# A recurrent attention block with routed rows: the order of scores and results, and who owns which PSUM banks

## The chip, the cores and the metric

The kernel runs on one core of a Trainium2 chip. The metric is the device time of one execution in microseconds. TensorE (PE) multiplies matrices and writes only to PSUM; VectorE (DVE) and ScalarE (ACT) read PSUM and work element by element; GpSimd (POOL) works element by element on SBUF; SyncE (SP) issues the transfers between HBM and SBUF. Each engine works through its own instructions in the order in which they were written, and waits when an operand or a buffer isn't ready.

## What is computed

Two blocks follow one another. The first is a recurrence over 768 steps for 4 batches and 8 heads of width 48. The second picks the 128 rows of highest score of each batch, sends them through a small network of two layers (384 to 1024 to 384) and adds the result, gated, to these rows.

```python
for t in range(S):
    kt, vt, rt, wt = (k[:, :, t], v[:, :, t], r[:, :, t], w[:, :, t])
    cur = np.einsum('bhd,bhe->bhde', u[None] * kt, vt)
    y[:, :, t] = np.einsum('bhd,bhde->bhe', rt, state + cur)
    state = wt[:, :, :, None] * state + np.einsum('bhd,bhe->bhde', kt, vt)
...
scores = np.einsum('bsd,d->bs', x, w_gate)      # x is y as (B, S, H*D)
out = x.copy()
for b in range(B):
    top_idx = np.argpartition(-scores[b], capacity)[:capacity]
    xe = x[b, top_idx]
    ye = np.maximum(xe @ w1, 0.0) @ w2
    g = 1.0 / (1.0 + np.exp(-scores[b, top_idx]))
    out[b, top_idx] = x[b, top_idx] + g[:, None] * ye
```

All data is fp32.

## The kernel before

**Chunks.** The 768 steps of a batch are cut into 6 chunks of 128, so there are N = 24 chunks, worked through one after the other. Within a chunk the recurrence becomes products of matrices: with the running products of the decays, r and k are scaled to R and K, "scores" are the products of K and R, "masked" leaves those of earlier steps, and the results are the masked scores times v plus R times the state at the chunk's start. The state is carried on to the next chunk of the batch with the products of k and v. The heads are handled as four pairs (HP = 4), two heads on the 128 partitions.

**Turns.** The program is written as turns, `turn(i)` for i from -2 to 24, in an order set by hand (`tc.manual_schedule()`). A turn works on several chunks: it makes R of chunk i+1, the decays and K's transposes of chunk i+2, masked scores and results of chunk i, rows of chunk i-1, and it compares the row scores of chunk i-2 with those of the batch so far. As each engine keeps the written order, an instruction that waits holds up everything of its engine that is written after it.

What a turn does, by name:

- `first_left`, `own_products`, `own_weights`, `own_values`, `own_results`: the term with u, for the step itself. Products on POOL; then, for each of 8 heads, a sum over 48 elements on ScalarE (L372), then times v on POOL and, for chunks 1 to 7, half of the heads on ScalarE (L385).
- `scaled` K (L349): VectorE takes K's transposes from PSUM and scales them.
- `compared(i-2)`: TensorE spreads a column of row scores into psW (ps_e, L533); VectorE compares with all earlier chunks of the batch (L535, longer with each chunk) and with the chunk itself (L539); ScalarE keeps the spread scores in "every" for later chunks (L544), except after the last chunk of a batch.
- `back(i)`: K turned back for the carry (L278), copied by ScalarE to kt (L414). Not for a batch's last chunk.
- `rows_back(i-1)`: the results turned back to rows (L278), copied by ScalarE to x (L452); `rows_out` adds the own term (POOL, L458) and stores the rows; `row_products` (POOL, L463) and `row_sums` (ScalarE, L468) give the row scores.
- `masked(i)` (VectorE, L404).
- `inputs_t(i+1, "R")` (L271) and `scaled` R on VectorE; `decays_t(i+2)` (L271 into psW).
- `range_check(i+2)` on ScalarE (L338); `carry_products(i)` (L488), for the first chunks copied by ScalarE to kvs (L494); `carry` makes the next state.
- `outputs_t(i)`: the results (L429, L437) into ps_yt, copied by ScalarE to yt (L442).
- `scores(i+1)` (L396) into psS, then `inputs_t(i+2, "K")` (L271).
- `scans(i+2)` on VectorE: running products of the decays from the right (L291) and the left (L302).

**The routed part.** When the last chunk of a batch has been compared, `mixture(b)` is taken up, a generator that stands in the turns' `mix(place=...)`: ranks (ps_r, L562), "picks" on VectorE (L580), "half" (ps_i, L587, the list of rows, then the gather of the rows), "mid" (the gathered rows transposed, ps_x, L611, copied to xeT), then the gate. The network itself is `forward`, of which `fed_in_turn` puts a few products (L647, L659) into each turn. The last batch's network stands behind the last turn, with TensorE almost alone.

**PSUM.** Of the 8 banks psW has one (decays, ps_e), psT two that are used in turn (transposes of R and K, back, rows, carry), psS two (scores), psV two (one tile for the results, and in between ps_r, ps_i and ps_x), and psM one (the network). A tile that is asked for from a pool waits until the readers of the tile that had its bank are done.

**Loads.** `loads(i+5)` at a turn's end asks for w, r, k and v some chunks ahead, into four buffers each, on SyncE's queue, on which the stores of rows stand too. The weights of the network come in seven pieces from turn 2 on.

Of the kernel before, what the change touches and what calls it, by code (L numbers as in the profile page):

```python
# [10 lines left out]
FP32 = mybir.dt.float32  # L11
# [7 lines left out]
L = 128  # L19
DP = 64  # L20
# [17 lines left out]
def kernel(  # L38
# [49 lines left out]

    AHEAD = S // L + 2

    FIRST = H * 5 // 8
    NDC = C // L
    NFC = F // L
# [11 lines left out]
    psW = ctx.enter_context(tc.tile_pool(name="psW", bufs=1, space=PSUM))  # L105
    psT = ctx.enter_context(tc.tile_pool(name="psT", bufs=2, space=PSUM))
    psS = ctx.enter_context(tc.tile_pool(name="psS", bufs=1, space=PSUM))
    psV = ctx.enter_context(tc.tile_pool(name="psV", bufs=1, space=PSUM))
    psM = ctx.enter_context(tc.tile_pool(name="psM", bufs=1, space=PSUM))

    chunks = [(b, ci) for b in range(B) for ci in range(NCH)]
# [5 lines left out]
    def crossed(j, q):  # L117
        return q ^ (j & 1)

    def half(q):  # L120
        return slice(DP * q, DP * q + DP)
# [296 lines left out]
    def outputs_t(t):  # L418

        n = t["n"]  # L420
        vt = v_bufs[n % NBUF]
        old = state.get(n)

        ps = psV.tile([L, 2, HP, L], FP32, tag="v", name="ps_yt")

        for j in range(HP):
            for c in (0, 1):
                q = crossed(j, c)
                nc.tensor.matmul(  # L429
                    ps[half(c), j % 2, j // 2, :], vt[:, 2 * j + q, :], t["sc"][:, q, j, :],  # L430
                    start=(j < 2), stop=(old is None), skip_group_check=True,
                )
        for j in range(HP if old is not None else 0):
            for c in (0, 1):
                q = crossed(j, c)
                rows = slice(DP * q, DP * q + DP)
                nc.tensor.matmul(  # L437
                    ps[DP * c:DP * c + D, j % 2, j // 2, :], old[rows, j, :],
                    t["R"][rows, j, :], start=False, stop=True, skip_group_check=True,
                )  # L440
        t["yt"] = lev.tile([L, 2, HP // 2, L], FP32, tag="yt", name="yt")
        nc.scalar.copy(out=t["yt"], in_=ps[:, :, 0:HP // 2, :])  # L442

    def rows_back(t, soon=False):
        y = dense(psT, "t", lambda j: t["yt"][0:DE, j % 2, j // 2, :], lambda j: crossed(j, 0))
        x = t["x"] = lev.tile([L, C], FP32, tag="x", name="x", bufs=3)
        xj = x.rearrange("p (j e) -> p j e", j=HP)
        if soon:
            vo = t.pop("vo").rearrange("p (j q) d -> p j (q d)", q=2)
            nc.vector.tensor_add(xj, y, vo)  # L450
        else:
            nc.scalar.copy(out=xj, in_=y)  # L452
# [28 lines left out]
    def carry_products(t):  # L481
        n = t["n"]
        if chunks[n][1] == NCH - 1:
            return
        t["kv"] = kv = psT.tile([L, HP, D], FP32, tag="t", name="ps_kv")
        for j in range(HP):
            for q in (0, 1):
                nc.tensor.matmul(  # L488
                    kv[half(q), j, :], t["kt"][:, j, q, :],
                    v_bufs[n % NBUF][:, 2 * j + q, 0:D], start=True, stop=True,  # L490
                )
        if n < AHEAD:
            t["kv"] = lev.tile([L, HP, D], FP32, tag="kvs", name="kvs")
            nc.scalar.copy(out=t["kv"], in_=kv)  # L494
# [22 lines left out]
    def compared(t):  # L517

        b, ci = chunks[t["n"]]
        if ci == 0:  # L520
            while len(against) > 1:
                mix()
            against[b] = (
                mod.tile([L, S - L], FP32, name="every", bufs=2),
                mod.tile([L, NCH, S], BF16, name="ahead", bufs=2),
                lost_bufs[b % 2],
            )
        every, ahead, lost = against[b]
        own = score[:, b, ci:ci + 1]
        lo, hi = ci * L, (ci + 1) * L  # L530

        ps = psW.tile([L, L], FP32, tag="w", name="ps_e")
        nc.tensor.transpose(ps, own.to_broadcast([L, L]), ident)  # L533
        if ci > 0:
            nc.vector.tensor_scalar(  # L535
                out=ahead[:, ci, 0:lo], in0=every[:, 0:lo], scalar1=own, scalar2=None,
                op0=ALU.is_ge, op1=ALU.add, accum_out=lost[:, ci, 0:1],
            )
        nc.vector.scalar_tensor_tensor(  # L539
            out=ahead[:, ci, lo:hi], in0=ps, scalar=own, in1=after_f,  # L540
            op0=ALU.is_ge, op1=ALU.mult, accum_out=lost[:, ci, 1:2],
        )
        if ci < NCH - 1:
            nc.scalar.copy(out=every[:, lo:hi], in_=ps)  # L544

    def mixture(b):

# [4 lines left out]


        every, ahead, lost = against[b]
        def room(shape, name):
            pool, tag = (psT, "t") if ended else (psV, "v")
            return pool.tile(shape, FP32, tag=tag, name=name)

        ps = room([L, NCH], "ps_r")
# [12 lines left out]
        for gi, (c0, n) in enumerate(groups):  # L572
# [9 lines left out]
                    op0=ALU.is_equal,  # L582
                )
            yield "half"
            ps = room([L, 2], "ps_i")
            for c in range(NCH):
                nc.tensor.matmul(  # L587
                    ps, pick[:, c, :], ids[:, b, c, :], start=(c == 0), stop=(c == NCH - 1)
# [45 lines left out]
    def forward(b, n, idx, xe, xeT, gate, gated):  # L634

        load_weights(len(weights) - NFC // 2)
        hid = mod.tile([L, NFC, L], FP32, name="hid")  # L640
        for f0 in range(0, NFC, 4):

            pool, tag = (psV, "v") if ended and f0 % 8 == 0 else (psM, "m")
            ps = pool.tile([L, 4, L], FP32, tag=tag, name="ps_h")
            for q in range(4):
                for dc in range(NDC):
                    nc.tensor.matmul(  # L647
                        ps[:, q, :], w1[:, dc, (f0 + q) * L:(f0 + q + 1) * L],
                        xeT[:, dc, :], start=(dc == 0), stop=(dc == NDC - 1),
                    )  # L650
                if q == 3:
                    nc.scalar.activation(out=hid[:, f0:f0 + 4, :], in_=ps, func=AF.Relu)  # L652
                yield q == 3

        load_weights(len(weights))
        pool, tag = (psV, "v") if b == B - 1 else (psM, "m")
        ps = pool.tile([L, C], FP32, tag=tag, name="ps_f")
        for fc in range(NFC):
            nc.tensor.matmul(  # L659
                ps, hid[:, fc, :], w2[:, fc, :], start=(fc == 0), stop=(fc == NFC - 1)  # L660
            )
            yield fc == NFC - 1
        while not gated:
            mix()
        ye = mod.tile([L, C], FP32, name="ye", bufs=2)
        nc.vector.scalar_tensor_tensor(  # L666
            out=ye, in0=ps, scalar=gate, in1=xe, op0=ALU.mult, op1=ALU.add
        )
        nc.gpsimd.indirect_dma_start(  # L669
            out=views[b][0:b + 1].rearrange("b s c -> (b s) c"),  # L670
            out_offset=bass.IndirectOffsetOnAxis(ap=idx[0:n, 0:1], axis=0),
            in_=ye[0:n], in_offset=None,
            bounds_check=(b + 1) * S - 1, oob_is_err=False,
        )
        yield True
# [5 lines left out]
    def step(f, n, *more):  # L681
        if 0 <= n < N:
            f(work.setdefault(n, dict(n=n)), *more)
# [38 lines left out]
    def turn(i):  # L722
        soon = i >= N - 1
        step(first_left, i + 1)
        if i < 1:
            step(scaled_aside, i + 1, "K", "right")
        step(own_products, i + 1)

        first = FIRST if feed or picked else 0
        step(own_values, i, range(first))  # L730
        step(carry, i - 1, work.get(i))
        if i > 0:
# [7 lines left out]
            sums.extend(check_sums())  # L740
        if i < N:
            step(compared, i - 2)
        step(back, i)
        step(rows_back, i - 1, soon)
        mix(place="half")
        if not soon:
# [13 lines left out]
        if i == -2:  # L760
            warm(2)
        step(range_check, i + 2)
        if not soon:
            step(row_sums, i - 1)
        if i == -1:
            spread(u_bc.rearrange("p h d -> p (h d)"), u_row)
            step(own_weights, i + 1)
        step(carry_products, i)
        step(outputs_t, i)
        step(scores, i + 1)  # L770
        step(inputs_t, i + 2, "K", k_bufs)
        if i == -2:
            warm(1)
# [3 lines left out]
        fed_in_turn(PIECES - PIECES // 2, 1 if i == N - 1 else 0)  # L777
        if i == N - 1:
            step(compared, i - 1)
        step(scans, i + 2)  # L780
        mix(place="end")
        if i > -2:
            loads(i + 5)
# [3 lines left out]
    with tc.manual_schedule():  # L787
        warm(6)
        for i in range(-2, N + 1):
            turn(i)  # L790

        ended.append(True)
        mix(1000)
        mixing.append([mixture(B - 1), "picks"])
        step(compared, N - 1)
        fed(1)
        mix(2)
        wide = checked(sums)
        fed(1)
        mix()  # L800
        fed(NFC - 2)
        mix(2)
        fed(2)
        mix(1000)
        fed(1000)
        outside = nc.values_load(wide, min_val=0, max_val=1)


    def general(gen):
        u_t = gen.tile([D, H], FP32, name="u_t")  # L810
        nc.sync.dma_start(out=u_t, in_=u.rearrange("h d -> d h"))
        for b in range(B):
# [27 lines left out]
            for c in range(NCH):  # L840
                x = lev.tile([L, C], FP32, tag="x", name="x", bufs=3)
                nc.sync.dma_start(out=x, in_=out[b, c * L:(c + 1) * L, :])
                t = dict(n=b * NCH + c, x=x)
                row_scores_soon(t)
                compared(t)
            for _ in mixture(b):
                pass
            fed(1000)
# [30 lines left out]
```

## Time and profile before

| | |
|---|---|
| time, median of 3 runs | 206.23 us (203.56 to 206.38) |
| profiled run | 204.75 us, span 203.0 us |
| left scan (L302) of turn 2, 5, 8, 11, 14, 17, 20 starts at | 26.75, 46.59, 67.41, 90.68, 112.63, 134.30, 156.25 us |
| busy: TensorE, VectorE, POOL, ScalarE | 184.6, 161.1, 139.5, 127.8 us |
| transfers of r, k, v, w, each chunk | 192 KB each, 4.2 to 5.0 us from issue to landing |

The left scan is the last step of VectorE in a turn, so the distance of two of these starts is the length of the turns between them. Batch 0's rows are ranked in turns 7 to 9; from then on the network's products stand in the turns. The last scan starts at 163.48 us; after the last turns the network of the last batch follows. A matrix product in the profile is pipelined with the next: four transposes of 280 ns each take 0.44 to 0.66 us together.

### The profile page before, as it was taken

What the parts mean: (1) busy time and instruction counts of PE and PEld (TensorE: products, weight loads), DVE (VectorE), ACT (ScalarE), POOL (GpSimd) and SP (SyncE); (2) the same over time, 40 slices, a digit from 0 to 9 for tenths busy, and PEclk for the clock granted to TensorE, in tenths of its full rate; (3) what the DMA queues carried; (4) which work ended last, traced back from release to release, by engine and by line L of the source; (5) the groups of instructions that cost most, each with busy time, mean ns of one, the idle gap of its engine ahead of it and who ended that gap; (6) DMA issues with size and microseconds to landing.
All of it is one profiled execution on the core that took longest, in us unless ns stands there. A gap on an engine that the chain in (4) does not pass through costs nothing. (4 is left out here: it accounts for less than half of the span.)

```text
span 203.0 us, 7183 instructions
## 1 busy us (share of the span) xinstructions
PE 184.6 (91%) x2673; PEld 151.2 (74%) x2673; DVE 161.1 (79%) x348; ACT 127.8 (63%) x653; POOL 139.5 (69%) x186
## 2 busy tenths in 40 slices
PE   7898889887998979999999999999999999899980
PEld 2577768665776859879787789888788798776940
DVE  6999898999999696898999888998999885861010
ACT  5486879877994485688674576678646758410300
POOL 8689888876886966876686889697667797111302
PEclk9999999999999799999999999999999999999999
DMA  7999999999999989699776875958973141111101
GB/s 117 163 166 153 148 191 199 242 190 240 194 210 218 253 179 175 163 212 157 163 153 93 179 158 131 183 120 123 157 156 91 30 119 44 39 42 42 39 8 44
DMA packets 105390, 28.86 MB, mean 142 GB/s; under 512 B 100482, under 2 KB 104580, under 8 KB 105348
## 3 DMA queue, kind: packets, MB, share of 16 engines
q1 hardware_dynamic: 104304, 26.65, 73.4%
q0 software_dynamic: 512, 1.57, 2.3%
q8 instruction: 23, 0.38, 0.9%
q14 instruction: 19, 0.16, 0.3%
q10 hardware_dynamic: 532, 0.10, 0.2%
HBM read 22.81 MB, written 5.51 MB: 139 GB/s over the span
## 5 line engine op out<-in xcount | busy, mean ns | idle before, releaser
L372 ACT ACTIVATE rk<-rk 128x48 f32<-128x48 f32 x192 | 44.1, 240 | 0.0
L372 ACT ACTIVATION_READ_ACCUMULATOR rk<-rk 128x1 f32 x192 | 37.8, 197 | 0.0
L458 POOL TENSOR_TENSOR x<-x,vo 128x384 f32<-128x384 f32 x22 | 22.1, 1006 | 20.1 <-ACT x L452 20.0
L302 DVE TENSOR_TENSOR_SCAN left<-ps_w,from_left 128x511 f32<-128x511 f32 x24 | 30.7, 1280 | 0.9
L404 DVE TENSOR_TENSOR sc<-ps_s,before_f 128x1024 f32<-128x1024 f32 x24 | 29.2, 1218 | 1.4 <-PE ps_s L396 1.4
L291 DVE TENSOR_TENSOR_SCAN right_buf<-ps_w,from_right 128x511 f32<-128x511 f32 x24 | 29.1, 1211 | 0.6 <-PE ps_w L271 0.6
L429 PE MATMUL ps_yt<-sc,v_buf 128*64 128x128 f32 x384 | 26.6, 282 | 0.7 <-ACT xeT L613 0.5
L647 PE MATMUL ps_h<-xeT,w 128*128 128x128 f32 x192 | 25.0, 278 | 1.2 <-ACT hid L652 1.2
L396 PE MATMUL ps_s<-R,K 64*64 64x128 f32 x768 | 25.5, 270 | 0.0
L364 POOL TENSOR_TENSOR rk<-rk,u_bc 128x384 f32<-128x384 f32 x24 | 24.0, 1000 | 1.2 <-DVE alls L297 0.7
L647 PEld LDWEIGHTS ps_h<-xeT,w 128*128 128x128 f32 x192 | 22.9, 192 | 2.4 <-ACT hid L652 1.9
L361 POOL TENSOR_TENSOR rk<-r_buf,k_buf 128x384 f32<-128x384 f32 x24 | 24.2, 1007 | 0.0
L659 PE MATMUL ps_f<-w,hid 128*128 128x384 f32 x64 | 23.5, 495 | 0.0
L463 POOL TENSOR_TENSOR scr<-x,wg_bc 128x384 f32<-128x384 f32 x22 | 22.1, 1003 | 1.7
L396 PEld LDWEIGHTS ps_s<-R,K 64*64 64x64 f32 x768 | 21.8, 133 | 1.2 <-issue 1.1
L429 PEld LDWEIGHTS ps_yt<-sc,v_buf 128*64 128x64 f32 x384 | 21.4, 141 | 1.8 <-ACT xeT L613 0.6
L544 ACT COPY every<-ps_e 128x128 f32<-128x128 f32 x20 | 5.3, 264 | 24.3 <-DVE ahead L539 24.3
L349 DVE TENSOR_TENSOR R<-ps_t,left 128x512 f32<-128x512 f32 x24 | 16.5, 688 | 5.0 <-issue 3.6
L349 DVE TENSOR_TENSOR K<-ps_t,right_buf 128x512 f32<-128x512 f32 x22 | 15.1, 687 | 6.3 <-PE ps_t L271 5.7
L381 POOL TENSOR_TENSOR vo<-v_buf,own 128x384 f32<-128x384 f32 (+1 forms) x24 | 17.7, 737 | 3.4 <-ACT rk L372 3.4
L271 PE MATMUL ps_t<-ident,r_buf 128*128 128x128 f32 x96 | 15.0, 279 | 5.3 <-ACT kt L414 4.5
L271 PEld LDWEIGHTS ps_t<-ident,r_buf 128*128 128x128 f32 x96 | 10.8, 141 | 9.0 <-ACT kt L414 6.8
(118 smaller groups left out, 368.7 us busy)
## 6 DMA issues: line engine op xcount, KB each, us to landing
k_buf<-in_k_dram SPq DMA_DIRECT2D x24, 192.0 KB, 4.8
r_buf<-in_r_dram SPq DMA_DIRECT2D x24, 192.0 KB, 5.0
v_buf<-in_v_dram SPq DMA_DIRECT2D x24, 192.0 KB, 4.2
out_dram<-x SPq DMA_DIRECT2D x24, 192.0 KB, 2.6
w_buf<-in_w_dram SPq DMA_DIRECT2D x23, 192.0 KB, 4.8
w<-in_moe_w_dram SPq DMA_DIRECT2D x3, 512.0 KB, 5.6
w<-in_moe_w_dram SPq DMA_DIRECT2D x4, 384.0 KB, 5.1
w_buf<-in_w_dram ACTq DMA_DIRECT2D x1, 96.0 KB, 3.2
```

Of the source, the lines that this page charges most:

```text
L271: nc.tensor.transpose(ps[:, j, :], src(j), ident)
L291: nc.vector.tensor_tensor_scan(out=flat[:, W - 2::-1], data0=wt[:, W - 1:0:-1], data1=from_right.rearrange("p j t -> p (j t)")[:, W - 2::- ...
L302: nc.vector.tensor_tensor_scan(out=left.rearrange("p j t -> p (j t)")[:, 1:W], data0=wt[:, 0:W - 1], data1=start.rearrange("p j t -> p (j ...
L349: nc.vector.tensor_mul(out, t.pop(name + "t"), t.pop(by))
L361: nc.gpsimd.tensor_mul(rk, r_bufs[n % NBUF][:, :, 0:D], k_bufs[n % NBUF][:, :, 0:D])
L364: nc.gpsimd.tensor_mul(t["rk"], t["rk"], u_bc)
L372: nc.scalar.activation(out=rk[:, h, :], in_=rk[:, h, :], func=AF.Copy, accum_out=o[:, h:h + 1])
L396: nc.tensor.matmul(ps[half(c), q, j, :], t["K"][half(q), j, half(c)], t["R"][half(q), j, :], start=True, stop=True,)
L404: nc.vector.tensor_mul(t["sc"].rearrange("p q j t -> p (q j) t"), ps.rearrange("p q j t -> p (q j) t"), _heads(before_f, 2 * HP),)
L429: nc.tensor.matmul(ps[half(c), j % 2, j // 2, :], vt[:, 2 * j + q, :], t["sc"][:, q, j, :], start=(j < 2), stop=(old is None), skip_group_ ...
L647: nc.tensor.matmul(ps[:, q, :], w1[:, dc, (f0 + q) * L:(f0 + q + 1) * L], xeT[:, dc, :], start=(dc == 0), stop=(dc == NDC - 1),)
L659: nc.tensor.matmul(ps, hid[:, fc, :], w2[:, fc, :], start=(fc == 0), stop=(fc == NFC - 1))
```

## The change

The change does several things that belong together:

- For the first nine chunks (n < LATE = 9) the results take no banks of their own: they are written into the scores' two banks, psS, after VectorE has read the scores. So the scores of the next chunk can't follow the results directly in those banks; they move to the front of the next turn (`step(scores, i)`), and K's transposes follow the results at once.
- The two banks of psV become two pools of one bank, psY and psK. In the first nine chunks psY holds the rows turned back and psK the carry's products, so that psT serves only back, R and K. In later chunks the results lie in psY and psK, one half each, with a copy for each half, and rows and carry are in psT as before.
- The copy of the spread scores to "every" becomes a step of its own, `kept`. In later turns it stands behind `back`, that is, behind the copy of kt on ScalarE; in the first turns it stays where it was.
- In the first turns five of the eight own values are placed at the turn's front, and the row sums stand behind the copy of the results.
- In the first turns batch 0's picks are placed at the end of the turn, behind the scans.
- Two products of zeros (`warm(2)`) stand ahead of ps_i when no product of the network is at hand, to keep TensorE active.

Cut to the core:

```diff
+    LATE = S // L + 3
...
-    psV = ctx.enter_context(tc.tile_pool(name="psV", bufs=1, space=PSUM))
+    psY = ctx.enter_context(tc.tile_pool(name="psY", bufs=1, space=PSUM))
+    psK = ctx.enter_context(tc.tile_pool(name="psK", bufs=1, space=PSUM))
...
     def outputs_t(t):
-        ps = psV.tile([L, 2, HP, L], FP32, tag="v", name="ps_yt")
+        if n < LATE:
+            both = psS.tile([L, 2, HP, L], FP32, tag="s", name="ps_yt")
+            ps = [both[:, o, 0:HP // 2, :] for o in (0, 1)]
+        else:
+            ps = [
+                pool.tile([L, HP // 2, L], FP32, tag=tag, name=f"ps_yt_{tag}")
+                for pool, tag in ((psY, "y"), (psK, "k"))
+            ]
...
-        nc.scalar.copy(out=t["yt"], in_=ps[:, :, 0:HP // 2, :])
+        if n < LATE:
+            nc.scalar.copy(out=t["yt"], in_=both[:, :, 0:HP // 2, :])
+        else:
+            for o in (0, 1):
+                nc.scalar.copy(out=t["yt"][:, o], in_=ps[o])
...
     def rows_back(t, soon=False):
-        y = dense(psT, "t", ...)
+        pool, tag = (psY, "y") if t["n"] + 1 < LATE else (psT, "t")
+        y = dense(pool, tag, ...)
...
     def carry_products(t):
-        t["kv"] = kv = psT.tile([L, HP, D], FP32, tag="t", name="ps_kv")
+        pool, tag = (psK, "k") if n < LATE else (psT, "t")
+        t["kv"] = kv = pool.tile([L, HP, D], FP32, tag=tag, name="ps_kv")
...
     def compared(t):
-        ps = psW.tile([L, L], FP32, tag="w", name="ps_e")
+        t["e"] = ps = psW.tile([L, L], FP32, tag="w", name="ps_e")
...
+    def kept(t):
+        b, ci = chunks[t["n"]]
+        ps = t.pop("e")
         if ci < NCH - 1:
-            nc.scalar.copy(out=every[:, lo:hi], in_=ps)
+            nc.scalar.copy(out=against[b][0][:, ci * L:(ci + 1) * L], in_=ps)
...
     def mixture(b):
             yield "half"
-            ps = room([L, 2], "ps_i")
+            if not (ended or feed or picked):
+                warm(2)
+            ps = room([L, 2], "ps_i", psK, "k")
...
     def turn(i):
         step(own_products, i + 1)
-        first = FIRST if feed or picked else 0
+        if i <= LATE:
+            step(scores, i)
+        first = FIRST if i < LATE or feed or picked else 0
         step(own_values, i, range(first))
...
             step(compared, i - 2)
+        if i < LATE:
+            step(kept, i - 2)
         step(back, i)
+        if LATE <= i < N:
+            step(kept, i - 2)
         step(rows_back, i - 1, soon)
...
         step(range_check, i + 2)
-        if not soon:
+        if i >= LATE and not soon:
             step(row_sums, i - 1)
...
         step(outputs_t, i)
-        step(scores, i + 1)
+        if i >= LATE:
+            step(scores, i + 1)
         step(inputs_t, i + 2, "K", k_bufs)
...
+        if i < LATE and not soon:
+            step(row_sums, i - 1)
         step(scans, i + 2)
+        if i < LATE:
+            mix(place="picks")
         mix(place="end")
```

More of the change, by code (lines that the diff above doesn't have):

```diff
@@ L429, in outputs_t @@
                 nc.tensor.matmul(
-                    ps[half(c), j % 2, j // 2, :], vt[:, 2 * j + q, :], t["sc"][:, q, j, :],
+                    ps[j % 2][half(c), j // 2, :], vt[:, 2 * j + q, :], t["sc"][:, q, j, :],
                     start=(j < 2), stop=(old is None), skip_group_check=True,
@@ L437, in outputs_t @@
                 nc.tensor.matmul(
-                    ps[DP * c:DP * c + D, j % 2, j // 2, :], old[rows, j, :],
+                    ps[j % 2][DP * c:DP * c + D, j // 2, :], old[rows, j, :],
                     t["R"][rows, j, :], start=False, stop=True, skip_group_check=True,
@@ L441, in outputs_t @@
         t["yt"] = lev.tile([L, 2, HP // 2, L], FP32, tag="yt", name="yt")
-        nc.scalar.copy(out=t["yt"], in_=ps[:, :, 0:HP // 2, :])
+        if n < LATE:
[3 more added lines that the diff above has]
+                nc.scalar.copy(out=t["yt"][:, o], in_=ps[o])
     def rows_back(t, soon=False):
-        y = dense(psT, "t", lambda j: t["yt"][0:DE, j % 2, j // 2, :], lambda j: crossed(j, 0))
+        pool, tag = (psY, "y") if t["n"] + 1 < LATE else (psT, "t")
+        y = dense(pool, tag, lambda j: t["yt"][0:DE, j % 2, j // 2, :], lambda j: crossed(j, 0))
         x = t["x"] = lev.tile([L, C], FP32, tag="x", name="x", bufs=3)
@@ L542, in compared, with room @@
         )
+    def kept(t):
+        b, ci = chunks[t["n"]]
+        ps = t.pop("e")
         if ci < NCH - 1:
-            nc.scalar.copy(out=every[:, lo:hi], in_=ps)
+            nc.scalar.copy(out=against[b][0][:, ci * L:(ci + 1) * L], in_=ps)
     def mixture(b):
         every, ahead, lost = against[b]
-        def room(shape, name):
-            pool, tag = (psT, "t") if ended else (psV, "v")
+        def room(shape, name, pool=psY, tag="y"):
+            if ended:
+                pool, tag = psT, "t"
             return pool.tile(shape, FP32, tag=tag, name=name)
@@ L641, in forward @@
         for f0 in range(0, NFC, 4):
-            pool, tag = (psV, "v") if ended and f0 % 8 == 0 else (psM, "m")
+            pool, tag = (psY, "y") if ended and f0 % 8 == 0 else (psM, "m")
             ps = pool.tile([L, 4, L], FP32, tag=tag, name="ps_h")
@@ L655, in forward @@
         load_weights(len(weights))
-        pool, tag = (psV, "v") if b == B - 1 else (psM, "m")
+        pool, tag = (psY, "y") if b == B - 1 else (psM, "m")
         ps = pool.tile([L, C], FP32, tag=tag, name="ps_f")
@@ L779, in turn @@
             step(compared, i - 1)
+            step(kept, i - 1)
+        if i < LATE and not soon:
+            step(row_sums, i - 1)
         step(scans, i + 2)
+        if i < LATE:
+            mix(place="picks")
         mix(place="end")
@@ L795 @@
         step(compared, N - 1)
+        step(kept, N - 1)
         fed(1)
@@ L845, in general @@
                 compared(t)
+                kept(t)
             for _ in mixture(b):
```

## The prediction

> **What bounds the kernel now.** I read the page first, then busy time by stretch (one stretch for each turn of the main loop, cut at the start of the left scan at L302), then the order of time in an ordinary early turn, then the waits.
>
> ```profile
> PE 184.6 (91%) x2673; PEld 151.2 (74%) x2673; DVE 161.1 (79%) x348; ACT 127.8 (63%) x653; POOL 139.5 (69%) x186
> ...
> PEclk9999999999999799999999999999999999999999
> ```
>
> TensorE looks like the bound, but 91% is an average over two different regimes. By turn (columns: PE, PEld, DVE, ACT, POOL busy, clock, DMA share, GB/s):
>
> ```profile
> 33.38:40.13 6.75, 5.69 (x113) 4.77 (x107) 5.93 (x11) 5.60 (x32) 5.50 (x8) 1.00 1.15 231
> ...
> 53.14:59.43 6.29, 6.02 (x117) 4.95 (x113) 6.19 (x11) 5.98 (x32) 5.36 (x7) 1.00 1.14 194
> 59.43:67.41 7.98, 6.64 (x92) 5.50 (x86) 7.53 (x18) 4.88 (x28) 5.63 (x7) 0.88 1.03 245
> 67.41:75.61 8.20, 6.75 (x104) 5.57 (x102) 6.05 (x13) 5.01 (x27) 5.83 (x8) 0.91 0.97 212
> ...
> 90.68:97.72 7.04, 7.04 (x117) 6.53 (x112) 6.29 (x11) 5.69 (x29) 5.49 (x7) 1.00 0.84 165
> 97.72:104.54 6.82, 6.82 (x103) 5.41 (x99) 6.50 (x12) 4.49 (x25) 4.92 (x7) 1.00 0.75 150
> ```
>
> From about 75 us TensorE is without a gap (7.04 of 7.04); only fewer products would help there. Before that it idles about 1 us a turn, and VectorE is the longest engine: 5.93 of 6.75 us in turn 4. Turn 7 (53.14 to 59.43) shows what an early turn can be: VectorE busy 6.19 of 6.29. It follows chunk 5, whose comparison has no copy of "every". An ordinary turn:
>
> ```profile
> 35.03 0.69 DVE L349 TENSOR_TENSOR K<-ps_t,right_buf 128x512 f32<-128x512 f32 x1 [0.37 <-PE ps_t L271]
> ...
> 36.30 1.22 DVE L404 TENSOR_TENSOR sc<-ps_s,before_f 128x1024 f32<-128x1024 f32 x1
> 36.42 0.27 ACT L544 COPY every<-ps_e 128x128 f32<-128x128 f32 x1 [1.15 <-DVE ahead L539]
> 36.58 0.48 ACT L414 COPY kt<-ps_t 128x384 f32<-128x384 f32 x1
> ...
> 37.12 0.42 PEld L271 LDWEIGHTS ps_t<-ident,r_buf 128*128 128x128 f32 x4 [0.89 <-ACT kt L414]
> ...
> 37.87 0.69 DVE L349 TENSOR_TENSOR R<-ps_t,left 128x512 f32<-128x512 f32 x1 [0.34 <-issue]
> ...
> 40.11 1.05 PE L396 MATMUL ps_s<-R,K 64*64 64x128 f32 x32
> ...
> 41.09 0.42 PEld L271 LDWEIGHTS ps_t<-ident,k_buf 128*128 128x128 f32 x4 [0.17 <-issue]
> ...
> 41.79 0.69 DVE L349 TENSOR_TENSOR K<-ps_t,right_buf 128x512 f32<-128x512 f32 x1 [0.37 <-PE ps_t L271]
> ```
>
> Two waits of VectorE repeat. Its K waits for K's transposes, which stand on TensorE behind 1 us of scores. Its R waits for R's transposes, these for a bank of psT, that for the kt copy on ScalarE, which stands behind "every", which waits for VectorE: ScalarE idles 1.15 us. In all turns:
>
> ```profile
> ACT every L544 <- DVE ahead L539: 24.3, 18, 2.8
> ...
> DVE K L349 <- PE ps_t L271: 5.7, 8, 1.7
> ...
> PE ps_t L271 <- ACT kt L414: 4.5, 8, 0.9
> ```
>
> Last, turn 8 to 9, where batch 0 is ranked and TensorE goes slack:
>
> ```profile
> 66.23 1.95 PE L429 MATMUL ps_yt<-sc,v_buf 128*64 128x128 f32 x16
> ...
> 70.63 0.69 DVE L349 TENSOR_TENSOR K<-ps_t,right_buf 128x512 f32<-128x512 f32 x1 [1.69 <-PE ps_t L271]
> ...
> 75.13 1.09 PE L429 MATMUL ps_yt<-sc,v_buf 128*64 128x128 f32 x16 [0.52 <-ACT xeT L613]
> ```
>
> The sixteen products take 1.95 us where they take 1.06 elsewhere: the clock means 0.88 and 0.91 leave (0.12 x 7.98 + 0.09 x 8.20)/0.5 = 3.4 us at half clock. K then waits 1.69 instead of 0.37 us.
>
> **What the Trainium skill says.** "TensorE: Matmul & The Clock Gate", Part 1, has a window of about 3.4 us after which an idle TensorE falls to half clock; the 3.4 us agree. The same page's table under the title calls VectorE and ScalarE strict FIFO; the trace agrees, kt sat behind "every". "PSUM — Partial Sum Buffer", Specifications, gives 8 banks of 512 fp32, and before uses all (1+2+2+2+1), so separate banks for carry and rows in early chunks must come from yt's pair: yt shares the scores' banks. "DMA: Bandwidth & Descriptors", Specifications, asks for 512 B transfers for full rate; here 100482 of 105390 packets are smaller, and the DMA is 99% busy to 65 us: a candidate for a limit.
>
> **The change part by part.** S(i) is the start of "masked" (L404) in turn i.
>
> Carry and rows in banks of their own (chunks below 9). psT is asked for 3 times a turn, not 5, in its two banks. R then takes the bank that K left at the start of the turn and waits for no kt. Its 0.35 us go in turns 2, 3, 4 and 6.
>
> Scores in front. K's transposes now follow the results directly, a microsecond earlier: 0.61, 0.38, 0.37 and 0.37 us of VectorE's wait go in turns 2 to 5; turns 6 and 7 have none to give. The cost is a new ring through psS: masked(i), results(i), the yt copy, scores(i+1), masked(i+1). Behind the waiting scores on TensorE stand ps_e, back and rows_back; VectorE's comparison waits for ps_e. From S: ScalarE does every, kt, x at starts of 0.12, 0.28, 0.65; three heads of own values instead of eight (0.227 each), four vo (0.90), the range check (0.60), kvs (0.20), so yt starts at 3.4 and ends at 4.0; scores 1.05, ps_e 0.3, then comparison 0.35: 5.8 us. TensorE's results end by S + 3.4 too (R, w, kv by 1.8, then 1.65).
>
> Five heads in front, row sums behind yt. ScalarE's 1.15 us of idle takes five own values (1.14 us). Its work is unchanged, about 5.6 us busy; with starts end to end it is .16+.37+.38+.68+.9+.6+.2+.6+.7+.2+1.14 = 5.9 us. POOL has 5.6 us (7 operations near 1.0, 0.5 or 0.6).
>
> So an early turn is the longest of VectorE, ScalarE 5.9 and the ring 5.8. VectorE from turn 7 is 6.29 with a five-block comparison (0.80); taking out the blocks: 5.5, 5.75, 5.9, 6.0, 6.15, 6.3 for turns 2 to 7. Before, S ran 16.56 (turn 1), 22.92 (2), 29.54 (3), 36.30 (4), 43.19 (5), 49.31 (6), 56.04 (7), 63.79 (8), 71.78 (9). After: turn 1 is short before (11.33 to 16.56) and becomes a ring turn, a light one without "every" or x, estimated at 5.6: S(1) = 16.9; then 22.8, 28.8, 34.7, 40.8 (turn 5: 6.0), 47.0, 53.3.
>
> Picks at the end of turn 7. 2.0 us of VectorE move from turn 8's front to turn 7's end, ahead of S(8) either way. S(8) = 53.3 + 5.5 + 2.05 + 0.16 = 61.0 (before 63.8). TensorE meanwhile has scores, back and rows to do.
>
> Two zero products. Not seen warm with 512 columns; cold they run at 0.38 to 0.46 us, six in 2.74. At full clock I halve: 0.2 each, 0.4 together, between 0.2 and 0.46; nothing is fed then, so they run once, beside VectorE. I take the half clock as gone in this stage (about 2 in 3): 1.3 us of K's wait.
>
> Turn 9. It has both scores(9) and scores(10), a microsecond that was only moved. ScalarE has eight own values and xeT before yt: S(9) = 61.0 + 5.95 = 67.0, yt(9) at S + 3.0 = 70.0. Before it started at 75.13: 5.1 us. I take off 0.8 for links between engines (turn 7 still loses 0.1), so 4.3.
>
> Late turns. yt goes through two banks and two copies: 192 columns take 303 and 384 take 484 ns, so 256 take about 0.36, two 0.72 instead of 0.58: +0.15 us on a ScalarE that is busy 4.5 to 5.7 of 7 us, hidden beside TensorE. "every" behind kt frees R earlier; TensorE idles 0.2 to 0.4 us in two turns of six: 0.4 us over the rest. The tail is unchanged. Sum 4.7: 206.2 - 4.7 = 201.5.
>
> **Rivals.**
> A: as worked out, 201.5. For it: turn 7. Chance 0.42.
> B: the early gain is halved, by the DMA or by the half clock coming back. Turns 2 to 8 move 7 x 0.98 MB and 2.4 MB of weights: 9.2 MB at 220 GB/s is 42 us, against 44 forecast for them, so it fits closely; loads land 4.8 us after issue and are used 3.5 us or more after that. Gain 2.2 to 2.9, 203.7. Chance 0.26.
> C: the runs of before spread from 203.6 to 206.4; if the high ones have more half clock than the profiled one (204.75), what steadies it is worth 2.5 us more: 199.0. Chance 0.20.
> D: the ring binds. Eight links with 0.15 us each on 5.8 us make 7.0 a turn against 6.5 in the mean before: 7 x 0.5 = +3.5, less 1.3 of clock: 208.4, slower. For it: four engines are within 0.5 us of each other in such a turn. Against: before also hands over between engines, and turn 7 runs at 98%. Chance 0.12, a third of it beyond 2%.
>
> **How the numbers follow.** The likeliest is A. Faster by over 2% means below 202.1: C, and two thirds of A with some of B, 0.55. Slower than 210.4: 0.05. The rest 0.40. The range leaves out the far ends of C and D: 198.5 to 205.5.
>
> **What would show it.** Right: K of VectorE no longer waits for ps_t and R no longer through kt; ScalarE's wait before "every" falls from 24 to under 15 us; S distances of 5.9 to 6.3 in turns 2 to 7; clock 1.00 in the stretch of batch 0's ranking; late turns unchanged at 6.7 to 8.1. Wrong: a new wait of PE ps_s for ACT yt that VectorE's masked inherits, loads that land after TensorE asks, or a half clock elsewhere.

## The result, and the profile after

| | before | changed |
|---|---|---|
| median time | 205.69 us (203.56 to 206.38, 4 runs) | 199.51 us (199.01 to 199.69, 4 runs) |
| ratio to before, 95% interval | | 0.9713 [0.9635, 0.979] |
| profiled run, span | 204.75, 203.0 us | 199.46, 197.8 us |

The changed kernel is faster by 2.9%. The times of the kernel before lie in groups near 203.4, 205.0 and 206.3 us; its profiled run is one of the middle group and has one stretch of half clock. So the two profiled runs, 204.75 and 199.46 us, are the pair to take apart: 5.3 us. Lines of the changed kernel lie some 6 to 30 further down; the names are the same.

The page of the changed kernel:

```profile
PE 183.4 (93%) x2674; PEld 149.9 (76%) x2675; DVE 160.3 (81%) x348; ACT 129.4 (65%) x668; POOL 139.4 (70%) x186
...
PEclk9999999999999999999999999999999999999998
```

The work is the same to within 2 us on each engine, in a shorter span; the 7 among the clock's nines is gone, and the 8 at the end is the idle tail. By turn (PE, PEld, DVE, ACT, POOL busy, clock, DMA share, GB/s):

```profile
32.21:38.05 5.84, 5.72 (x104) 4.79 (x103) 5.74 (x11) 5.67 (x31) 5.46 (x8) 1.00 1.18 228
...
56.37:64.44 8.07, 7.56 (x132) 6.12 (x131) 7.83 (x19) 4.65 (x26) 5.98 (x7) 1.00 1.16 231
64.44:70.41 5.97, 4.92 (x79) 3.90 (x78) 5.87 (x13) 4.75 (x26) 5.89 (x8) 1.00 1.19 237
...
92.59:99.41 6.82, 6.82 (x103) 5.41 (x99) 6.50 (x13) 4.54 (x26) 4.92 (x7) 1.00 0.89 185
```

The turn that was 6.75 us with VectorE busy 5.93 is 5.84 with VectorE busy 5.74: it is now full. Turn 9 fell from 8.20 to 5.97. The late turn is 6.82 us in both. The same early turn in order of time:

```profile
33.41 0.67 DVE L355 TENSOR_TENSOR K<-ps_t,right_buf 128x512 f32<-128x512 f32 x1
...
34.66 1.22 DVE L410 TENSOR_TENSOR sc<-ps_s,before_f 128x1024 f32<-128x1024 f32 x1
34.77 0.27 ACT L568 COPY every<-ps_e 128x128 f32<-128x128 f32 x1 [0.17 <-DVE ahead L558]
34.79 0.46 PEld L277 LDWEIGHTS ps_t<-ident,r_buf 128*128 128x128 f32 x4
34.94 0.48 ACT L420 COPY kt<-ps_t 128x384 f32<-128x384 f32 x1
...
35.79 0.68 DVE L355 TENSOR_TENSOR R<-ps_t,left 128x512 f32<-128x512 f32 x1
...
37.93 0.42 PEld L277 LDWEIGHTS ps_t<-ident,k_buf 128*128 128x128 f32 x4 [0.18 <-issue]
...
38.71 0.86 PEld L402 LDWEIGHTS ps_s<-R,K 64*64 64x64 f32 x32 [0.36 <-ACT yt L456]
```

Neither K nor R on VectorE shows a wait. R's transposes start at 34.79, ahead of the kt copy that they used to wait for; K's stand ahead of the scores; and the scores wait 0.36 us for the copy of the results, the new ring, without VectorE noticing. ScalarE's 1.15 us ahead of "every" became 0.17. Over the whole kernel its wait there fell from 24.3 to 6.2 us, but that is less than it seems: in the late turns the copy of kt now stands ahead of "every" and waits in its place, 15.3 us in all against 4.0 before. In the turns up to S(9) the wait fell from 7.9 to 4.0 us.

Where the 5.3 us come from, by S(i), the start of "masked" in turn i. "Masked" stands in the middle of its turn; below, the length of turn n is the distance from S(n-1) to S(n).

| from, to | before | changed | gained |
|---|---|---|---|
| start, S(1) | 16.56 | 16.75 | -0.2 |
| S(1), S(7) | 39.48 | 36.23 | 3.25 |
| S(7), S(8) | 7.75 | 8.07 | -0.3 |
| S(8), S(9) | 7.99 | 5.97 | 2.0 |
| S(9), S(10) | 8.26 | 7.88 | 0.4 |
| S(10), S(23) | 91.82 | 91.47 | 0.35 |
| S(23), end | 31.2 | 31.4 | -0.2 |

The first and the last line lie within the spread: S(1) is at 16.4 to 16.8 us in the profiles of the changed kernel and its variants, and the stretch behind S(23), whose work the change leaves alone, takes 31.1 to 31.4 us in all fourteen profiles.

### The profile page after: what moved, and what is told of

Read it like the earlier page. It is cut to its first block, busy times and chain, and to the rows that moved or that the text cites. A ratio compares the mean times of both kernels' runs of the same rounds, so it can differ in the third digit from the quotient of the medians.

```text
span 197.8 us, 7207 instructions
## 1 busy us (share of the span) xinstructions
PE 183.4 (93%) x2674; PEld 149.9 (76%) x2675; DVE 160.3 (81%) x348; ACT 129.4 (65%) x668; POOL 139.4 (70%) x186
## 4 chain that ended last, share of the span: by engine, by line
PE 65%; ACT 11%; DMA 8%; SPq 5%; DVE 5%; issue 2%; POOL 0%; POOLq 0%; DVEq 0%
PE ps_h L674 11%; PE ps_f L686 11%; PE ps_s L402 9%; PE ps_t L277 7%; SPq L157 5%; PE ps_t L284 5%; PE ps_kv L507 4%; PE ps_yt_y L442 4%; PE ps_yt_y L450 3%; PE ps_w L277 3%; DMA v_buf<-in_v_dram 3%; PE ps_yt_k L442 3%; DMA k_buf<-in_k_dram 3%; ACT rk L378 3%; DMA r_buf<-in_r_dram 2%; ACT vo L391 2%
## 5 line engine op out<-in xcount | busy, mean ns | idle before, releaser
L476 POOL TENSOR_TENSOR x<-x,vo 128x384 f32<-128x384 f32 x22 | 22.1, 1005 | 17.3 <-ACT x L470 17.1
L420 ACT COPY kt<-ps_t 128x384 f32<-128x384 f32 x20 | 9.6, 480 | 15.4 <-PE ps_t L284 15.3
L355 DVE TENSOR_TENSOR R<-ps_t,left 128x512 f32<-128x512 f32 x24 | 16.4, 685 | 3.1 <-issue 2.2
L486 ACT ACTIVATE scr<-scr 128x384 f32<-128x384 f32 x22 | 11.5, 525 | 9.9 <-POOL scr L481 9.7
L277 PE MATMUL ps_t<-ident,k_buf 128*128 128x128 f32 x96 | 15.7, 286 | 0.2 <-DMA k_buf<-in_k_dram 0.2
L277 PE MATMUL ps_w<-ident,w_buf 128*128 128x128 f32 x96 | 15.1, 281 | 0.6 <-ACT every L568 0.4
```

Of the source, the lines that this page charges most:

```text
L277: nc.tensor.transpose(ps[:, j, :], src(j), ident)
L355: nc.vector.tensor_mul(out, t.pop(name + "t"), t.pop(by))
L476: nc.gpsimd.tensor_add(x, x, t.pop("vo").rearrange("p h d -> p (h d)"))
```

## The experiments

The theory on record: VectorE bounds the early turns, two waits of it go (K by the order, R by the banks), the ring costs nothing as long as ScalarE is early, and the zero products keep the clock up. The rivals: the waits turn into others, the ring or the loads bind, or the clock alone is the gain. The medians of before, run beside each group, were 205.0 us (first four), 204.95 us (next four) and 206.1 us (last four), so comparisons among kernels are made within a group or by S distances.

**Without the zero products.**

```diff
-            if not (ended or feed or picked):
-                warm(2)
```

> The changed kernel (199.5 us) without the two zero products ahead of ps_i. If these products are what keeps the clock up in turns 8 and 9: 3.4 us at half clock return there, VectorE's K in turn 9 waits over 1 us more, about 200.8 us. If the new order alone leaves no slack window on TensorE: clock 1.00 there as in the changed kernel, 199.1 to 199.6 us (two products of at most 0.4 us beside VectorE's picks).

Measured: 198.85 us, ratio 0.9694 [0.9653, 0.9735], clock 1.00 until the tail. The changed kernel doesn't need them: the rest of the change leaves no half clock without them.

**Only the zero products, in the kernel before.**

```diff
             yield "half"
+            if not (ended or feed or picked):
+                warm(2)
             ps = room([L, 2], "ps_i")
```

> The kernel before (205.7 us) with the two zero products ahead of ps_i and nothing else. If they keep the clock up: no half clock between 60 and 75 us, VectorE's wait for K in turn 9 falls from 1.69 to about 0.4 us, 204.4 us. If TensorE's idle time around the copies of kt is what counts, the half clock stays and so does the time, 205.7 us.

Measured: 203.55 us, ratio 0.9933 [0.9914, 0.9952]. The order of time in its turns 8 and 9:

```profile
66.02 1.06 PE L429 MATMUL ps_yt<-sc,v_buf 128*64 128x128 f32 x16
69.17 0.69 DVE L349 TENSOR_TENSOR K<-ps_t,right_buf 128x512 f32<-128x512 f32 x1
```

The products that took 1.95 us take 1.06, K's wait of 1.69 us is gone, and the clock row of its page has no digit below 9 ahead of the tail. S(8) to S(9) is 6.40 against 7.99 us. So in the kernel before the half clock cost 1.5 us, and two zero products are enough against it in 17 of the 22 executions (203.1 to 203.6 us); the other five lie above 204.6 us. S(1) to S(7) is 39.48 us as before: this part is apart from the early turns.

**Only the scores in front.**

```diff
+    LATE = S // L + 3
...
+        if i <= LATE:
+            step(scores, i)
...
-        step(scores, i + 1)
+        if i >= LATE:
+            step(scores, i + 1)
```

> The kernel before with the scores of the first nine turns moved to the turn's front and nothing else: the results keep psV, rows and carry keep psT. If the scores ahead of K's transposes cause VectorE's wait for K: the waits of 0.61, 0.38, 0.37 and 0.37 us in turns 2 to 5 go, R still waits 0.35 us a turn for kt, 204.0 us. If the wait only moves (scores, ps_e and back now delay each other in front): 205.7 us.

Measured: 201.75 us, ratio 0.9832 [0.9792, 0.9872]. S(1) to S(7) is 37.78 us: 1.70 gained, where the four waits of K add up to 1.73. Its waits in all turns:

```profile
PE ps_t L272 <- ACT kt L415: 4.3, 9, 0.9
DVE R L350 <- issue: 4.0, 10, 0.4
DVE K L350 <- PE ps_t L272: 2.2, 3, 1.2
```

K's wait fell from 5.7 to 2.2 us. Of the 5.7, 1.73 lay in the early turns and 1.69 in the stretch of half clock; both are gone. The 2.2 us that are left lie behind S(9), S(15) and S(21), as before. R's wait and that for kt stayed, as the theory says. The rest of its gain is that its profile too has no half clock: S(8) to S(9) is 6.12.

**Only the rows in a bank apart.**

```diff
+    LATE = S // L + 3
...
-        y = dense(psT, "t", ...)
+        pool, tag = (psM, "m") if t["n"] + 1 < LATE else (psT, "t")
+        y = dense(pool, tag, ...)
```

> The kernel before with the rows turned back into psM (which the network doesn't use yet) instead of psT for the first nine turns, so that R's transposes take the bank that K left and not the one that kt has; order as before. If the bank is what makes R wait: the 0.35 us of VectorE's idle ahead of R go in turns 2, 3, 4 and 6, K's wait stays, 204.3 us. If the wait for K takes it up: 205.7 us.

Measured: 200.73 us, ratio 0.979 [0.9747, 0.9833], more than either reading said. S(1) to S(7) is 36.86 us: 2.62 gained, not 1.4. Its waits:

```profile
DVE R L350 <- issue: 2.6, 6, 0.5
DVE K L350 <- PE ps_t L272: 2.5, 4, 1.2
...
PE ps_t L272 <- ACT kt L415: 1.3, 3, 0.5
```

The scores still stand ahead of K's transposes, and yet K's waits in turns 3 to 5 fell from 1.12 us together to 0.26, all of it in turn 4. In turn 2 the wait grew, from 0.61 to 0.90 us. R's transposes are ahead of all of a turn's later products on TensorE; when they wait for kt, everything behind them is late, K's transposes last. So in turns 3 to 5 most of K's wait was the same delay seen a second time. The profile has no half clock either: S(8) to S(9) is 5.96 us, with TensorE's order as before.

**Both, without the ring.** The two edits together in the kernel before: the results keep their own banks.

> The kernel before with both: scores in front in the first nine turns and rows turned back into psM. The results keep psV, so there is no ring through the scores' banks; own values, row sums, picks, zero products and every as before. If the two waits of VectorE are the early gain: S distances of 5.5 to 6.3 us in turns 2 to 7 as in the changed kernel, 205.7 - 3.1 = 202.6 us. If ScalarE's idle time ahead of every (own values not in front) binds: S distances stay above 6.3, 204 us or more.

Measured: 200.04 us, ratio 0.9748 [0.969, 0.9807]. S(1) to S(7) is 35.83 us: 3.65 gained. The two alone give 1.70 and 2.62, 4.3 together: they overlap by 0.7 us. VectorE sets the turns without five own values in front and with ScalarE still waiting for "every"; that idle time cost nothing. The changed kernel has 3.25: ring and loads take back 0.4, most of it in turn 2 (6.28 against 5.97 us). But S(7) to S(8) is 9.69 us here, with 3.4 us of half clock: TensorE's ps_r stands in the results' banks and waits 1.35 us for their copy. Not every execution has this clock: three took 199.6 to 199.8 us with a mean clock of 0.990 to 0.998, three 200.3 to 201.4 us with 0.985 to 0.988.

**Own values back.**

```diff
-        first = FIRST if i < LATE or feed or picked else 0
+        first = FIRST if feed or picked else 0
```

> The changed kernel with all eight own values behind the rows' copy in the first nine turns, none in front. Five of them (1.14 us) then stand ahead of the copy of the results: by the sum of the prediction the ring through psS becomes 5.8 + 1.1 = 6.9 us a turn against 5.8 to 6.2 measured, about 5 us in turns 2 to 7, 204.5 us. If the ring has more slack than that sum: 199.5 to 200.5 us.

Measured: 203.78 us, ratio 0.9953 [0.993, 0.9975]. The turns 3, 4, 5 and 7 take 6.84, 6.84, 6.86 and 6.84 us, one length whatever the comparison's size, against 5.79 to 6.24: the ring binds, at the sum of its links. Turn 6, in which the copies of kt and kvs drop out of it (0.37 and 0.20 us), takes 6.26. Its waits:

```profile
PEld ps_s L402 <- ACT yt L456: 9.1, 8, 2.0
PE ps_s L402 <- ACT yt L456: 7.4, 8, 1.8
```

The same waits are 3.3 and 0.9 us in the changed kernel. So the five own values in front are no gain by themselves (the kernel without a ring does without them); they pay for sharing the scores' banks.

**"every" ahead of kt in late turns.**

```diff
-        if i < LATE:
+        if i < N:
             step(kept, i - 2)
         step(back, i)
-        if LATE <= i < N:
-            step(kept, i - 2)
```

> The changed kernel with the copy of every ahead of kt in the late turns too, as in the kernel before. If late turns are bound by TensorE without a gap: 199.5 to 199.9 us. If kt's place on ScalarE decides when R is ready there: +0.2 to 0.3 us in each of 14 turns, 202.5 to 203.5 us.

Measured: 199.63 us, ratio 0.9719 [0.9665, 0.9772]. Eleven of the distances from S(9) on are the same to 0.01 us; three differ, those that end at S(10), S(16) and S(22), with 8.25, 7.71 and 7.71 us against 7.88, 7.53 and 7.53: 0.73 us together. With "every" first, the copy of kt ends 0.76 instead of 0.59 us behind S(15) and S(21), R's transposes wait 0.36 instead of 0.19 us for its bank, and TensorE starts the results 0.18 us later. Behind S(9) R's transposes wait 0.60 us where the changed kernel has no such wait, and the results, held by xeT in both, start after 3.35 instead of 2.98 us. The other late turns are TensorE's. The changed kernel was not run beside this one, so these distances say more than its median.

**Gathered rows in psM.**

```diff
-            ps = room([L, NDC, L], "ps_x")
+            ps = room([L, NDC, L], "ps_x", psM, "m")
```

> The changed kernel with the gathered rows transposed into psM instead of psY, so that turn 9's results (and those of turns 15 and 21) don't wait for ScalarE's copy xeT. If TensorE's 0.86 us of idle time there lies on the path: 198.6 us. If VectorE or ScalarE take it up: 199.5 us.

Measured: 198.3 us, ratio 0.9655 [0.9602, 0.9708]. S(9) to S(10) is 6.82 instead of 7.88 us; two later turns are 7.65 instead of 7.53. TensorE's wait for xeT lay on the path.

**The changed kernel again**, for the next three.

> The changed kernel as it is, beside the next three on the same chip: 199.0 to 199.7 us, half clock between 55 and 75 us in none of its profiles.

Measured: 198.98 us (198.71 to 199.5), ratio 0.9669 [0.963, 0.9708]. S(7) to S(8) is 7.78 here, against 8.07 in the first profile.

**Picks in front, no zero products.**

```diff
-        if i < LATE:
-            mix(place="picks")
         mix(place="end")
```

together with the first edit.

> The changed kernel with the picks at turn 8's front again and without the zero products. If it is the place of the picks that keeps TensorE's window full (scores, back and rows run beside them), the half clock returns in part or all of the executions, 200.3 us or a spread of over 1 us. If the order of scores alone does it: 198.9 to 199.6 us, as VectorE's sum is the same.

Measured: 198.55 us (198.16 to 199.22), ratio 0.9648 [0.9608, 0.9687]; the clock is full in its profile. Neither part has a gain here that can be measured, and neither is what ends the half clock.

**Only batch 0's gathered rows in psM.**

```diff
-            ps = room([L, NDC, L], "ps_x")
+            ps = room([L, NDC, L], "ps_x", *((psM, "m") if b == 0 else (psY, "y")))
```

> The changed kernel with only batch 0's gathered rows transposed into psM, the others in psY. With all batches in psM turn 9 gave 1.06 us and turns 15 and 21 took 0.12 us each: 0.24 us below that kernel, 1.0 to 1.1 us below the changed one, about 198.1 to 198.4 us. If the loss in turns 15 and 21 was not from psM: 198.3 to 198.5 us.

Measured: 197.94 us (197.12 to 198.23), ratio 0.9606 [0.9566, 0.9646], the best of all: 1.0 us below the changed kernel on the same chip, with no overlap of their runs. Turn 9's results start 1.95 us behind S(9) here, and 2.98 us behind it in the changed kernel. The first line is from this kernel, the second from the changed one:

```profile
68.60 0.41 PE L442 MATMUL ps_yt_y<-sc,v_buf 128*64 128x128 f32 x4
```

```profile
70.00 0.44 PE L442 MATMUL ps_yt_y<-sc,v_buf 128*64 128x128 f32 x4 [0.86 <-ACT xeT L640]
```

**Combined.** The kernel without a ring, with the late order of "every", picks at the end, zero products, and batch 0's gathered rows in psM.

> The kernel before with scores in front, rows in psM in early turns, results in psV throughout (no ring), and with the later parts of the change: every behind kt in late turns, picks at the turn's end, zero products; and batch 0's gathered rows in psM. Early turns of 5.7 to 6.2 us without the ring's 0.4 us and turn 9 short: 0.4 below the preceding kernel, about 197.8 us. If one copy of 512 columns in late turns or the missing own values in front cost: 198.2 us or more.

Measured: 201.18 us, ratio 0.977 [0.9728, 0.9813]: a miss by over 3 us. S(1) to S(7) is 35.99, as hoped for. S(9) to S(10) is 7.36, better than before but not the 6.82 of the preceding kernel. And S(7) to S(8) is 10.97. The clock on its page, and TensorE's order of time in turns 7 and 8:

```profile
PEclk9999999999995899999999999999999999999999
```

```profile
57.78 0.66 PE L568 MATMUL ps_r<-minus,ahead 128*128 128x1 bf16 x21 [1.53 <-ACT yt L443]
...
62.30 1.01 PE L257 MATMUL ps_n<-nothing 128*128 128x512 bf16 x2 [1.05 <-ACT x L454]
```

The ranks wait 1.53 us for the copy of the results, whose banks they share, and the zero products, put into psM where the rows now are, wait 1.05 us for the rows' copy and hold ps_i behind them. TensorE runs dry twice and is at half clock from 59.6 to 66.4 us. The products meant to keep it busy became a wait by the bank that they were given. The half clock is not the whole of the miss: three of the six executions have a mean clock of 0.990 to 0.997 and still took 200.6 to 200.8 us, near 3 us above what was hoped for. That this rest is the two waits is read from the profile alone; no run takes either of them away.

## Why the prediction was right

The forecast was 201.5 us in 198.5 to 205.5, faster; measured are 199.51 us, inside the range and 2.0 us below the likeliest value. The mechanism of the early turns was right; that the range held is in part owed to its width. By its steps:

- *VectorE bounds the early turns.* Right. The S that it worked out against those measured: 16.9 (16.75), 22.8 (23.03), 28.8 (28.82), 34.7 (34.66), 40.8 (40.63), 47.0 (46.74), 53.3 (52.98), 61.0 (61.05), 67.0 (67.02), and the results of turn 9 at 70.0 (70.00). From S(8) on so close a match is luck: in the second profile of the same kernel S(7) to S(8) is 0.3 us shorter. Turn 2 is the exception, 6.28 instead of 5.9: there a load of v lands after 6.2 us, ps_kv waits 0.48 us for it, and the delay goes through the ring. The chain of the changed kernel, from that load on, and in turn 4:

```profile
12.16 6.22 DMA v_buf<-in_v_dram
18.51 0.67 PE ps_kv L507 x16
19.18 0.89 PE ps_yt L442 x16
20.07 0.63 PE ps_yt L450 x16
20.72 0.59 ACT yt L456
21.36 1.10 PE ps_s L402 x32
...
36.48 0.89 ACT vo L391 x4
37.37 0.60 ACT junk L344 x2
38.17 0.49 ACT yt L456
38.71 1.10 PE ps_s L402 x32
```

  Rows, own values, vo, the range check, yt, scores: the ring that was added up beforehand is what the chain walks through. It lies within 0.2 us of VectorE's own sum.
- *The size of the ring, 5.8 us, and 6.9 with all own values behind.* Confirmed at 6.84 us. The links as they were listed add up to 5.7, not 5.8 us; with 1.14 us for five own values that is the 6.84 measured.
- *Which edit removes which wait.* Right for the order (1.73 by the waits, 1.70 measured), wrong for the banks: 1.4 was counted, 2.62 measured, because R's wait delays all that TensorE does afterwards. The sum for both was right only because it was taken from VectorE's work and not from adding waits.
- *The half clock in turns 8 and 9, 1.3 us.* Its size was right (1.5 by the zero products alone). Its cause stays open. The zero products suffice in most executions of the kernel before, but the rest of the change does it without them, and in their profiles so do the scores in front alone and the bank for the rows alone; with these two together it is there in half of the executions. The place of the picks is not it. Idle time of TensorE, which the prediction took for the cause, doesn't decide it alone, and the 3.4 us that it found to agree are the length of the half clock, not of an idle stretch: in the 3.4 us ahead of the half clock TensorE is busy for 2.45 us in the kernel before (62.1 to 65.5), for 2.05 us in the one with both edits (54.8 to 58.2) and for 1.87 us in the combined one (56.2 to 59.6), but between 53.5 and 56.9 us of the kernel with the own values back for only 1.71 us, and its profile has no half clock there. Nor does the wait of ps_r for the results' banks: 0.39, 1.35 and 1.53 us in the three whose profiles show the half clock, 1.12 us in the one with only the scores in front, which shows none.
- *0.8 us for links between engines.* Mis-sized: there was nothing to take off, S(9) is exact without it. VectorE is busy 98% of turns 3 to 7.
- *0.4 us in the late turns.* Right in its path and nearly in its size: S(15) to S(16) and S(21) to S(22) are 0.18 us shorter each, by R's transposes and kt. The 0.37 us between S(9) and S(10) lie ahead of turn 9's results and were already in the 5.1.
- *The start.* This is the larger error. The sum was read from a profiled run of 204.75 us, but taken off the median of 206.2; that makes 1.45 of the 2.0 us. The rest is the sum itself: 5.3 us between the profiled runs, 4.7 forecast, mostly the 0.8 for links. The kernel before has three groups of times, and the mean clocks of its 65 executions beside the experiments follow them: 0.994 to 0.995 up to 203.7 us, 0.985 to 0.990 from 204.6 to 205.4, 0.980 to 0.982 above 205.8. The 3.4 us at half clock in its profile take 0.008 off such a mean (0.5 x 3.4 / 203), so by this estimate the groups have no, one and two such stretches. Rival C was right in this, and its 199.0 us is nearer to the measurement than the 201.5 of A.

Rival B (loads) shows in turn 2 alone, 0.4 us. The DMA column that the prediction read as 99% busy adds up the times of packets and goes above 1 (1.18 in the changed kernel's turn of 5.84 us), so a value near 1 doesn't show a limit. Rival D (the ring binds) is what happens when five own values are moved. Not tried alone were the row sums behind yt and the late results in two banks.

## What to carry to other kernels

Add up the engine that is busiest in a stage, and each closed ring of buffers by its links; in this kernel the larger was the turn. Don't add up waits: two waits on one in-order engine can be one delay seen twice, as here 1.7 and 2.6 us gave 3.65. A bank that is shared binds all who use it to the slowest reader, also small products that stand in it only now and then: a free bank for ps_x was worth 1.0 us, and in a busy one two zero products waited 1.05 us themselves.

## What the runs showed of the hardware

Picks, 128 x 128 in bf16, take 243 ns in the median, but one of 24 took 1036 ns, beside a POOL multiplication that ended at 59.59 us:

```profile
L605 DVE TENSOR_SCALAR pick<-slots,rank x24: 240/243/1036, 58.0 to 175.5; 128x128 bf16<-128x128 bf16 x24
...
58.60 0.99 POOL L370 TENSOR_TENSOR rk<-rk,u_bc 128x384 f32<-128x384 f32 x1
```

The Trainium skill, "SBUF — State Buffer", Who interferes with whom, says that VectorE, where it runs in a mode that uses two ports, as instructions of this kind can, shares a pair of ports with GpSimd, and that whichever issued first holds the pair for its whole instruction while the other is blocked. The traces agree in time: each long pick ends about 0.05 us behind the POOL operation beside it, in the kernel before as well (825 ns), while the last batch's six, with no POOL work beside them, take 254 ns at most. That ports are the reason no run here shows. In the changed kernel and its variants S(7) to S(8) follows the number of picks held in this way: with one of about 1005 ns it is 7.8 us, with two 8.1 (the changed kernel's first profile), with three 8.4 ("every" ahead of kt). With the picks in front one is held, for 749 ns, and the distance is 7.6. The fp32 multiplications of VectorE from PSUM beside POOL's in the same turn kept their 0.68 us.
